# A fold of two weight matrices woven into attention: matmuls issued in pieces, sums moved out of PSUM later

## The chip, the cores and the metric

The kernel runs on one core of a Trainium2 chip. The core has five engines, each with its own in-order queue: TensorE (PE in the profile; PEld is its weight load), VectorE (DVE), ScalarE (ACT), GpSimd (POOL) and SyncE (SP), which issues the transfers here. TensorE writes its sums into PSUM, which ScalarE and VectorE read; all else is kept in SBUF. The metric is the device time of one execution in microseconds (us).

## The reference

The kernel computes three stages in a row on 2304 tokens of width 512.

```python
scores = scale * q @ k.T           # 4 batches x 8 heads, 576 tokens, head width 64, causal
a = softmax(scores)                # over the keys
local = a @ v
mem_out = (phi(q) @ M_prev) / (phi(q) . z_prev + 1e-6)
x = g * mem_out + (1 - g) * local  # g: one gate per head
x = ((x @ w1) * (x @ w2)) @ w3 @ w_out     # 512 -> 1024 -> 1024 -> 512
h = x @ w_in                               # 512 -> 2048
x = (h - tanh(h)) @ w_out2                 # 2048 -> 512
```

The weights w1, w2, w3, w_out, w_in and w_out2 arrive as 64-bit numbers.

## The kernel before

**Decoding.** A tile of weights is loaded as 64-bit words (`dec_load`) and turned into fp32 by `dec_ops`: one ScalarE pass (L74), four VectorE passes (L75, L77, L81, L84), and then a split into a high and a low part by two GpSimd passes (L96, L99). Products of fp32 accuracy are made of three matmuls: high by high, high by low, low by high. `Decoder` hands out such a tile in five pieces, one for each call of `step`, and issues the load of a later tile when one is done.

**The fold.** Since nothing stands between w3 and w_out, the kernel multiplies them first: `fold_work` makes WF = w3 @ w_out while attention runs. It decodes eight tiles of w_out (`o`) and 16 tiles of w3 (`zs`, eight for each half of the 1024 rows). For each of eight row blocks and each half, 12 matmuls of 512 columns add into one PSUM bank (`fo`). In the first half ScalarE copies the sum to SBUF (`part`, L291). In the second half VectorE adds that part (`s`, L294), ScalarE copies the rounded sum (`wf`, L296) and VectorE subtracts to get the low part (L297). The bank comes from the pool `psA`, whose two banks attention's outputs (`o`, in `av`) use too.

**Attention.** There are 80 units: 16 pairs of heads, five blocks of queries each. The outer loop (`for m in range(NU + 8)`) issues for each step, in the order of ORDER, the scores, exponentials and normalization of unit m (S, E, N), the transposes of unit m - 1 (T), some preparation of the next pair (L), the background work (G, three steps behind), and the outputs (A, two steps behind, after the second and the fifth unit of a pair).

**Background work.** `early()` is a generator that runs the fold, and then the first memory group (`mem_group(0)`) interleaved with the decoding of the first four tiles of w1 and w2: after each memory step come two decoder steps. G gives it a budget: BG = 2.13 in the first 40 steps and BG2 = 2.09 in the others are added to a counter, and each piece that is not a `yield 1` takes one from it. The fold yields 1 after each three matmuls, so these cost nothing and the 12 matmuls of a fold are issued within one step, with the sum's way out of PSUM right behind them. Eight pieces are issued before the first step.

The framework that the kernel is written in takes this order as a priority. It places each instruction on its engine's queue when a simulation of the timeline finds it ready, so pieces of the background can be issued a little ahead or behind; on the chip each engine then keeps to its queue's order.

**After attention.** The products with w1 and w2 (`ab`) and with WF (`x`) follow in six groups of 384 tokens, beside the other memory groups and the rest of the decoding, and then the third stage in the same groups.

Of the kernel before, what the change touches and what calls it, by code (L numbers as in the profile page):

```python
# [11 lines left out]
F32 = mybir.dt.float32  # L12
# [5 lines left out]
AF = mybir.ActivationFunctionType  # L18
ALU = mybir.AluOpType
# [13 lines left out]
def block_kernel(ctx, tc, qk, qt, vt, mp, zp_d, beta, w1, w2, w3t, wo, wi, wo2, ident_d, mask_d, out):  # L33
    nc = tc.nc
    PE, DV, AC, PO, SP = nc.tensor, nc.vector, nc.scalar, nc.gpsimd, nc.sync
# [3 lines left out]
    wfp = ctx.enter_context(tc.tile_pool(name="wfp", bufs=1))  # L39
# [15 lines left out]
    def wslot(pool, tag, dt=F32R):  # L55
        return pool.tile([128, 2, 512], dt, tag=tag, name=tag if dt == F32R else tag + "p")
# [110 lines left out]
    OP, FL = 5, "V"  # L167
    SN, XP, MR = 2, (), 0
    TH = (("V", 0), ("A", 0))
    PS = 1  # L170
    U1 = 2
    NE, EM, BG = 4, 1, 2.13
    BG2, MB = 2.09, 40
    MS, FS, FS5 = 4, 3, 12
    CPA = (0, 1, 3, 4)

# [57 lines left out]
    WF = {}  # L234
# [16 lines left out]

    def fold_item(f, half):
        def dst():
            t = wslot(ap1, "zs")
            fv[f, half] = t
            return t[:, 0], t[:, 1]

        r = slice(512 * half, 512 * half + 512)
        return w3t[r, f * 128:f * 128 + 128].rearrange("(k p) c -> p k c", p=128), dst

    def fold_work(psum):
        seq = [("o", j) for j in range(4)]
        for f in range(8):
            if f >= OP:
                seq += [("o", 4 + f - OP)] if 4 + f - OP < 8 else []
            seq.append((f, 0))
        seq += [("o", j) for j in range(12 - OP, 8)]
        for f in range(8):
            seq += [("x", i) for i, x in enumerate(XP) if x == f]
            seq.append((f, 1))  # L270
        make = {"o": fold_o_item, "x": lambda i: w_items[i]}
        dec = Decoder([make[k[0]](k[1]) if k[0] in make else fold_item(*k) for k in seq], DW, 3)
        part = {}
        for half in range(2):
            for f in range(8):
                while dec.done <= seq.index((f, half)) or half and dec.done <= seq.index(("o", 7)):
                    dec.step()
                    yield
                acc = psum()
                t = fv.pop((f, half))  # L280
                for j in range(4):
                    o = FO[4 * half + j]
                    c = slice(128 * j, 128 * j + 128)
                    mm(acc, t[:, 0, c], o[:, 0], j == 0, False)
                    mm(acc, t[:, 0, c], o[:, 1], False, False)
                    mm(acc, t[:, 1, c], o[:, 0], False, j == 3)
                    if j % FG == FG - 1:
                        yield 1
                if half == 0:
                    part[f] = wslot(wfp, f"wf{f}", F32)  # L290
                    AC.activation(out=part[f][:, 0], in_=acc, func=AF.Copy)  # L291
                else:
                    s = ap1.tile([128, 512], F32, tag=f"s{f % SN}", name="s")
                    DV.tensor_tensor(out=s, in0=acc, in1=part[f][:, 0], op=ALU.add)  # L294
                    WF[f] = wslot(wfp, f"wf{f}")
                    AC.activation(out=WF[f][:, 0], in_=s, func=AF.Copy)  # L296
                    (DV if FL == "V" else PO).tensor_tensor(out=WF[f][:, 1], in0=s, in1=WF[f][:, 0].bitcast(F32),  # L297
                                                            op=ALU.subtract)
                    yield 2

    if True:
        load_qk(0)
# [336 lines left out]
        def do(x, n):  # L639
            nonlocal pp  # L640
            if not 0 <= n < NU:
                return
            P, u = units[n]
            if x == "S":
                if u == 0 and P >= 2:
                    run(pp)
                for y in range(2):
                    scores(n, y)
                    rmax(n, y)
            elif x == "E":  # L650
                for y in range(2):
                    exps(n, y)
            elif x == "N":
                norm(n)
            elif x == "T":
                trans(n)
            elif x == "A" and u in (1, 4):
                av(P, u // 4)
                if u == 4 and P + 2 < 16:
                    load_v(P + 2)  # L660
            elif x == "L":
                if u == 0 and P >= 1:
                    run(pp)
                    pp = prep_qk(P + 1) if P + 1 < 16 else iter(())
                for _ in range(PS):
                    next(pp, None)
            elif x == "G":
                bgc[0] += BG if n < MB else BG2
                with ExitStack() as s:
                    for e, k in TH:  # L670
                        if n - k >= 0:
                            s.enter_context(tc.issue_after(mark[e][n - k]))
                    while bgc[0] >= 1:
                        if next(bg, None) != 1:
                            bgc[0] -= 1

        for m in range(NU + 8):
            for x in ORDER:
# [361 lines left out]
```

## Time and profile before

The median of three runs is 1062.15 us (1060.85 to 1065.14). The profiled execution took 1062.19 us; its span, from the first to the last instruction, is 1060.4 us, and the mean granted TensorE clock 0.975 of full speed.

| engine | busy us | share of the span | instructions |
|---|---|---|---|
| TensorE | 987.8 | 93% | 5512 |
| TensorE weight load | 860.3 | 81% | 5512 |
| VectorE | 821.7 | 77% | 1465 |
| ScalarE | 609.5 | 57% | 1413 |
| GpSimd | 442.4 | 42% | 446 |

Busy time is the union of an engine's instructions, averaged over stages with different limits. Matmuls overlap, so TensorE's busy time isn't its work at full speed. A wait is put down to the instruction that released it last.

### The profile page before, as it was taken

The numbers are of one execution on the slowest core, as the hardware profiler recorded it, in microseconds if no ns is written. First come the engines' busy times: TensorE is split into PE (matmuls) and PEld (weight loads), VectorE is DVE, ScalarE is ACT, GpSimd is POOL, SyncE is SP. The second block draws the span as 40 slices with busy tenths as digits, with TensorE's granted clock in tenths as the row PEclk, the third lists the DMA queues.
The fourth block names the chain that finished last, engine by engine and source line by source line (L and its number), as shares of the span: only waits on it lengthen the run. The fifth ranks groups of instructions, "written<-read, shape, count | busy, mean of one in ns | idle before, by whom it ended". The sixth has DMA issues, their size and how long they took to land.

```text
span 1060.4 us, 15816 instructions
## 1 busy us (share of the span) xinstructions
PE 987.8 (93%) x5512; PEld 860.3 (81%) x5512; DVE 821.7 (77%) x1465; ACT 609.5 (57%) x1413; POOL 442.4 (42%) x446
## 2 busy tenths in 40 slices
PE   5799898978899899999999997999999999999998
PEld 3476666655588789999999987789999999999996
DVE  7989998999879995467121498988778787787875
ACT  5577676666732432324121534777777776776764
POOL 5788777778646423100000584622222222222221
PEclk8699999998999899999999998999999999999999
DMA  9764675543324451125000022000000000000000
GB/s 246 182 174 123 173 196 136 135 126 95 94 73 152 137 177 50 41 88 160 1 1 1 20 74 86 1 1 30 1 1 30 1 31 1 1 31 1 31 1 30
DMA packets 44415, 77.73 MB, mean 73 GB/s; under 512 B 5168, under 2 KB 30000, under 8 KB 42416
## 3 DMA queue, kind: packets, MB, share of 16 engines
q1 hardware_dynamic: 44336, 76.73, 26.0%
q8 instruction: 43, 0.70, 0.3%
q14 instruction: 36, 0.29, 0.1%
HBM read 72.00 MB, written 4.72 MB: 72 GB/s over the span
## 4 chain that ended last, share of the span: by engine, by line
PE 66%; DVE 22%; POOL 6%; issue 4%; ACT 2%; DMA 1%; SPq 0%; DVEq 0%; POOLq 0%; ACTq 0%
PE o L143 20%; PE h L143 18%; PE ab L143 14%; PE x L143 7%; DVE T L81 3%; PE sc L143 2%; DVE T L75 2%; DVE T L84 2%; DVE st L394 2%; POOL p L427 2%; DVE qs L224 2%; PE t L459 1%; DVE T L77 1%; DVE ks L226 1%; PE fo L143 1%
## 5 line engine op out<-in xcount | busy, mean ns | idle before, releaser
L922 POOL TENSOR_TENSOR gl<-s,gh 128x384 fp32r<-128x384 f32 x96 | 102.0, 1062 | 286.0 <-ACT gh L916 267.7
L427 POOL TENSOR_SCALAR p<-p,st 128x128 f32<-128x128 f32 (+2 forms) x144 | 111.6, 787 | 52.2 <-DVE st L420 25.5
L143 PE MATMUL ab<-xh,wa 128*128 128x384 f32 x384 | 109.8, 343 | 5.0 <-DVE a L723 2.0
L143 PE MATMUL ab<-xh,wb 128*128 128x384 f32 x384 | 108.5, 340 | 2.8 <-POOL wb L96 2.0
L143 PE MATMUL x<-abh,wf 128*128 128x384 f32 x384 | 108.4, 343 | 1.6 <-ACT abh L726 1.6
L143 PE MATMUL sc<-ks,qs 128*128 128x256 f32 (+4 forms) x384 | 92.0, 358 | 18.2 <-DVE qs L224 9.5
L898 DVE SCALAR_TENSOR_TENSOR s<-s,u 128x384 f32<-128x384 f32 x96 | 82.2, 857 | 23.6 <-ACT s L888 22.8
L407 ACT ACTIVATE p<-sc,st 128x256 f32<-128x256 f32 (+4 forms) x160 | 82.6, 527 | 31.2 <-DVE st L394 13.3
L723 DVE TENSOR_TENSOR a<-ab,a 128x384 f32<-128x384 f32 x48 | 26.5, 553 | 86.2 <-PE ab L143 73.5
L894 ACT ACTIVATE u<-u,pc 128x384 f32<-128x384 f32 x96 | 59.3, 620 | 43.6 <-DVE s L898 43.5
L143 PEld LDWEIGHTS sc<-ks,qs 128*128 128x128 f32 x384 | 63.3, 205 | 25.5 <-ACT p L407 9.6
L74 ACT ACTIVATE T<-raw 128x512 f32<-128x512 f32 x72 | 48.8, 678 | 55.9 <-POOL wb L99 9.2
L143 PEld LDWEIGHTS ab<-xh,wa 128*128 128x128 f32 x384 | 70.5, 189 | 10.0 <-issue 3.3
L904 DVE TENSOR_TENSOR t<-h,t 128x384 f32<-128x384 f32 x96 | 53.1, 553 | 30.1 <-ACT t L887 29.7
L143 PEld LDWEIGHTS ab<-xh,wb 128*128 128x128 f32 x384 | 71.1, 190 | 4.5 <-POOL wb L96 2.7
L459 PE MATMUL t<-ident,p 128*128 128x128 f32 x320 | 54.6, 291 | 21.4 <-POOL p L427 8.2
L143 PEld LDWEIGHTS x<-abh,wf 128*128 128x128 f32 x384 | 71.3, 191 | 2.9 <-ACT abh L726 2.5
L903 DVE SCALAR_TENSOR_TENSOR s<-s,s 128x384 f32<-128x384 f32 x96 | 65.5, 682 | 7.9
L886 ACT ACTIVATE u<-h 128x384 f32<-128x384 f32 x96 | 46.8, 488 | 40.8 <-PE h L143 40.8
L143 PE MATMUL x<-abl,wf 128*128 128x384 f32 x192 | 65.6, 341 | 3.3 <-DVE abl L727 3.3
L143 PE MATMUL h<-xh,wf 128*128 128x384 f32 x240 | 67.5, 342 | 1.0 <-DVE s L905 1.0
L96 POOL TENSOR_SCALAR wb<-T 128x512 fp32r<-128x512 f32 x12 | 8.5, 709 | 142.4 <-PE ab L143 134.5
(205 smaller groups left out, 2865.0 us busy)
## 6 DMA issues: line engine op xcount, KB each, us to landing
r<-in_qk SPq DMA_DIRECT2D x30, 576.0 KB, 7.4
raw<-in_wo SPq DMA_DIRECT2D x24, 512.0 KB, 3.6
raw<-in_w3t SPq DMA_DIRECT2D x16, 512.0 KB, 4.9
raw<-in_w SPq DMA_DIRECT2D x16, 512.0 KB, 3.7
raw<-in_wi SPq DMA_DIRECT2D x16, 512.0 KB, 3.7
v<-in_vt SPq DMA_DIRECT2D x16, 320.0 KB, 6.0
mw<-in_qt SPq DMA_DIRECT2D x18, 256.0 KB, 3.0
out<-ob SPq DMA_DIRECT2D x18, 256.0 KB, 2.3
```

What stands on the lines that cost most here:

```text
L74: AC.activation(out=tf, in_=hw.bitcast(F32), func=AF.Abs)
L81: DV.scalar_tensor_tensor(out=l16, in0=lw, scalar=2.0 ** -29, in1=l16, op0=ALU.mult, op1=ALU.add)
L143: return PE.matmul(o, lhsT, rhs, start=start, stop=stop).ins
L407: mark["A"][n] = AC.activation(out=p_t[n][:, o:o + w], in_=sc_t.pop((n, x))[:, 0:w], func=AF.Exp, bias=st[:, b:b + 1], accum_out=st[:, 2 + ...
L427: (DV if NV[u] == "V" else PO).tensor_scalar(out=pr, in0=pr, scalar1=sc, scalar2=1.0, op0=ALU.mult, op1=ALU.mult)
L459: PE.transpose(t[:, m], p[:, K * h + 128 * kb:K * h + 128 * kb + 128], ident)
L886: AC.activation(out=u, in_=o, func=AF.Square)
L894: AC.activation(out=u, in_=u, func=AF.Relu, bias=pc[:, 2:3])
L898: DV.scalar_tensor_tensor(out=s1, in0=s1, scalar=k2[0], in1=u, op0=ALU.add, op1=ALU.mult)
L903: DV.scalar_tensor_tensor(out=s1, in0=s2, scalar=k2[1], in1=s1, op0=ALU.add, op1=ALU.mult)
L904: DV.tensor_tensor(out=t, in0=o, in1=t, op=ALU.subtract)
L922: PO.tensor_tensor(out=l, in0=s1, in1=h[:].bitcast(F32), op=ALU.subtract)
```

## The change

The fold's matmuls, still yielding 1 after each three, now take half a unit of the budget each, and one more piece follows the last of them. A sum is no longer taken out of PSUM right behind its matmuls: it is put on a list (`behind`), and `leave_step` issues one instruction of the oldest entry after each later decoder step: the copy of the first half is one such step, the add, the rounded copy and the subtract of the second half are three. When the decoding is over, the rest of the list is issued one piece at a time. The decoded w3 tile `zs` comes from a pool of two buffers (`ap2`) instead of one. Both budgets rise to 2.75. `mem_setup`, called at `yield 2`, now runs once, at the end of the fold.

```diff
--- before.py
+++ after.py
@@ -169,8 +169,8 @@
     TH = (("V", 0), ("A", 0))
     PS = 1
     U1 = 2
-    NE, EM, BG = 4, 1, 2.13
-    BG2, MB = 2.09, 40
+    NE, EM, BG = 4, 1, 2.75
+    BG2, MB = 2.75, 40
     MS, FS, FS5 = 4, 3, 12
     CPA = (0, 1, 3, 4)
 
@@ -251,7 +251,7 @@
 
     def fold_item(f, half):
         def dst():
-            t = wslot(ap1, "zs")
+            t = wslot(ap2, "zs")
             fv[f, half] = t
             return t[:, 0], t[:, 1]
 
@@ -271,10 +271,30 @@
         make = {"o": fold_o_item, "x": lambda i: w_items[i]}
         dec = Decoder([make[k[0]](k[1]) if k[0] in make else fold_item(*k) for k in seq], DW, 3)
         part = {}
+        behind = deque()
+
+        def leave(half, f, acc):
+            if half == 0:
+                part[f] = wslot(wfp, f"wf{f}", F32)
+                AC.activation(out=part[f][:, 0], in_=acc, func=AF.Copy)
+                return
+            s = ap1.tile([128, 512], F32, tag=f"s{f % SN}", name="s")
+            DV.tensor_tensor(out=s, in0=acc, in1=part[f][:, 0], op=ALU.add)
+            yield
+            WF[f] = wslot(wfp, f"wf{f}")
+            AC.activation(out=WF[f][:, 0], in_=s, func=AF.Copy)
+            yield
+            DV.tensor_tensor(out=WF[f][:, 1], in0=s, in1=WF[f][:, 0].bitcast(F32), op=ALU.subtract)
+
+        def leave_step():
+            if behind and next(behind[0], behind) is behind:
+                behind.popleft()
+
         for half in range(2):
             for f in range(8):
                 while dec.done <= seq.index((f, half)) or half and dec.done <= seq.index(("o", 7)):
                     dec.step()
+                    leave_step()
                     yield
                 acc = psum()
                 t = fv.pop((f, half))
@@ -286,17 +306,12 @@
                     mm(acc, t[:, 1, c], o[:, 0], False, j == 3)
                     if j % FG == FG - 1:
                         yield 1
-                if half == 0:
-                    part[f] = wslot(wfp, f"wf{f}", F32)
-                    AC.activation(out=part[f][:, 0], in_=acc, func=AF.Copy)
-                else:
-                    s = ap1.tile([128, 512], F32, tag=f"s{f % SN}", name="s")
-                    DV.tensor_tensor(out=s, in0=acc, in1=part[f][:, 0], op=ALU.add)
-                    WF[f] = wslot(wfp, f"wf{f}")
-                    AC.activation(out=WF[f][:, 0], in_=s, func=AF.Copy)
-                    (DV if FL == "V" else PO).tensor_tensor(out=WF[f][:, 1], in0=s, in1=WF[f][:, 0].bitcast(F32),
-                                                            op=ALU.subtract)
-                    yield 2
+                yield
+                behind.append(leave(half, f, acc))
+        while behind:
+            leave_step()
+            yield
+        yield 2
 
     if True:
         load_qk(0)
@@ -671,8 +686,7 @@
                         if n - k >= 0:
                             s.enter_context(tc.issue_after(mark[e][n - k]))
                     while bgc[0] >= 1:
-                        if next(bg, None) != 1:
-                            bgc[0] -= 1
+                        bgc[0] -= 0.5 if next(bg, None) == 1 else 1
 
         for m in range(NU + 8):
             for x in ORDER:
```

## Rows read from the trace of the kernel before

**Rows 1.** Busy time by stretch: PE, PEld, DVE, ACT, POOL, clock, DMA.

```profile
...
52.60:230.00 177.40, 158.23 (x1040) 117.31 (x1039) 166.70 (x343) 121.86 (x344) 139.82 (x154) 0.98 0.59 151
200.00:250.00 50.00, 40.29 (x259) 28.83 (x260) 49.72 (x94) 32.68 (x92) 38.55 (x39) 0.93 0.49 120
230.00:285.00 55.00, 45.98 (x321) 31.84 (x321) 52.43 (x124) 42.37 (x126) 41.13 (x51) 0.94 0.43 113
300.00:400.00 100.00, 91.53 (x510) 81.30 (x509) 90.08 (x161) 37.35 (x75) 46.03 (x38) 0.95 0.45 137
500.00:550.00 50.00, 50.00 (x288) 50.00 (x287) 10.74 (x20) 11.40 (x24) 0.00 (x0) 1.00 0.00 1
...
```

**Rows 2.** Waits of VectorE, 52.6 to 230 us: total us, times, longest.

```profile
...
DVE g L440 <- PE t L466: 3.0, 2, 1.8
DVE st L394 <- PE sc L143: 2.0, 2, 1.5
DVE ks L226 <- POOL ks L208: 1.8, 4, 1.2
...
DVE st L416 <- ACT p L407: 1.1, 2, 0.7
```

**Rows 3.** Groups of VectorE, 52.6 to 230 us: busy us, mean ns, idle before.

```profile
...
L84 DVE SCALAR_TENSOR_TENSOR T<-raw,T 128x512 uint32<-128x512 uint32 x21 | 17.9, 853 | 0.1
L81 DVE SCALAR_TENSOR_TENSOR T<-raw,T 128x512 uint16<-128x512 uint32 x21 | 16.9, 802 | 0.0
...
L75 DVE TENSOR_SCALAR T<-T 128x512 f32<-128x512 f32 x21 | 12.1, 574 | 1.5 <-ACT T L74 1.3
...
L77 DVE TENSOR_SCALAR T<-T 128x512 uint32<-128x512 uint32 x21 | 11.2, 531 | 0.1
...
L297 DVE TENSOR_TENSOR wf<-s,wf 128x512 fp32r<-128x512 f32 x7 | 5.4, 766 | 0.3
...
L294 DVE TENSOR_TENSOR s<-fo,wf1p 128x512 f32<-128x512 f32 x1 | 0.7, 673 | 0.0
...
```

**Rows 4.** Groups of TensorE, same stretch: the fold's matmuls and attention's outputs.

```profile
...
L143 PE MATMUL o<-g,v 128*64 128x320 f32 (+4 forms) x274 | 32.6, 368 | 1.0 <-DVE g L440 0.9 <-ACT g L438 0.2
...
L143 PE MATMUL fo<-z,zs 128*128 128x512 f32 x96 | 26.1, 414 | 1.1 <-POOL zs L99 0.6 <-POOL zs L96 0.4
...
L143 PE MATMUL fo<-wa,zs 128*128 128x512 f32 x48 | 16.0, 425 | 6.6 <-POOL zs L96 4.4 <-DVE mst L562 2.1
L143 PE MATMUL fo<-wb,zs 128*128 128x512 f32 x48 | 14.0, 400 | 0.0
...
```

**Rows 5.** Timeline, 160 to 170 us: start, us, engine, what, idle before.

```profile
...
160.16 2.48 POOL L427 TENSOR_SCALAR p<-p,st 128x256 f32<-128x256 f32 x4 [1.35 <-PE sc L143]
...
162.61 0.61 POOL L96 TENSOR_SCALAR zs<-T 128x512 fp32r<-128x512 f32 x1
...
163.28 0.82 PE L143 MATMUL fo<-wa,zs 128*128 128x512 f32 x2 [2.81 <-POOL zs L96]
...
164.99 0.69 DVE L440 COPY g<-t 128x512 f32<-128x512 f32 x1 [1.76 <-PE t L466]
...
```

**Rows 6.** Waits of ScalarE, 145 to 230 us.

```profile
...
ACT wf L296 <- DVE s L294: 10.8, 7, 2.4
...
```

**Rows 7.** Timeline of TensorE, 273 to 300 us.

```profile
...
274.38 2.16 PE L143 MATMUL o<-g,v 128*64 128x320 f32 x16
...
285.18 2.42 PE L143 MATMUL o<-g,v 128*64 128x320 f32 x20
...
291.90 0.44 PE L143 MATMUL ab<-xh,wa 128*128 128x384 f32 x1
...
```

**Rows 8.** Durations ns, min/median/max: the fold's subtract; GpSimd's second split pass.

```profile
...
L297 DVE TENSOR_TENSOR wf<-s,wf x8: 669/680/1100, 161.3 to 234.5; 128x512 fp32r<-128x512 f32 x8
...
L99 POOL TENSOR_TENSOR zs<-T,zs x16: 1267/1290/1648, 51.1 to 216.2; 128x512 fp32r<-128x512 f32 x16
...
```

**Rows 9.** DMA issues: count, KB each, us from issue to landing.

```profile
...
raw<-in_w3t SPq DMA_DIRECT2D x16, 512.0 KB, 4.9
...
```

## The prediction

> **What bounds the kernel now.** I read four views in this order. First the page's busy times, then busy time by stretch, because the page's average hides that the stages have different limits. From 500 us on TensorE is busy 50.00 of 50 us and VectorE only 10.74 [rows 1]: whatever happens earlier moves the end one for one, and nothing of the change lies in that part. The changed code (the fold and what is scheduled with it) runs from 52.6 to 230 us. There VectorE is busy 166.70 of 177.40 us, TensorE 158.23, ScalarE 121.86, GpSimd 139.82; from 230 to 285 us, where attention ends beside the first decoding of w1 and w2 and the first memory group, VectorE is busy 52.43 of 55.00 [rows 1]. So VectorE sets the pace until about 285 us, TensorE is close behind it, and the time there is VectorE's work plus VectorE's idle time: 10.7 us idle in the fold's stretch (177.40 - 166.70), 2.6 us after it. From 300 to 400 us TensorE is busy 91.53 and VectorE 90.08 of 100 us; that stage gets the same work either way.
>
> Second, the waits of VectorE in the fold's stretch. What a fold can cause is 3.0 us for copies `g` behind transposes and 2.0 us for row maxima `st` behind scores, 5.0 us together; the 1.8 us behind GpSimd's `ks` and 1.1 us behind an exponential have nothing of the fold in them [rows 2]. Third, the operations themselves: four VectorE passes for each decoded tile, and for the second half of the fold one add (0.7 us) and one subtract (0.766 us) [rows 3]; the fold's own matmuls, 26.1 + 16.0 + 14.0 = 56.1 us of TensorE, with idle time before them of 1.1 + 6.6 + 0 = 7.7 us, most of it ended by GpSimd's `zs` [rows 4]. Fourth, one such stall in order of time, to see whether it reaches VectorE: GpSimd normalizes from 160.16 us (2.48 us), so the split of `zs` starts only at 162.61, the fold's first two matmuls wait 2.81 us at the head of TensorE's queue, and the transposes queued behind them come late, so that VectorE's copy at 164.99 waits 1.76 us [rows 5]. That is the chain that the change can cut.
>
> **How often each thing is issued.** The background work gets a budget for each attention step (80 steps). Before: 2.13 units (2.09 later), five units a decoded tile, the fold's matmuls free. 24 tiles are 120 units, 8 are spent ahead, so the fold ends (112 - 40 x 2.13) / 2.09 = 12.8 steps after the first 40: about step 53 of the background, 56 in the outer count. Between the first fold (outer step 11) and the last (56) lie 45 steps, 177.4 / 45 = 3.94 us each. After: each fold costs 4 x 0.5 + 1 = 3 units more, 16 x 3 = 48, so (168 - 8) / 2.75 = 58.2 steps, outer step 61. The rest (18 rounds of one memory step and two decoder steps, 54 units, and three units for the last sum) takes 57 / 2.75 = 20.7 steps instead of 54 / 2.09 = 25.8, so both end at outer step 82. Walking the counters by hand, the last two matmul pieces of the first memory group are issued at steps 78 and 80 instead of 77 and 79. Nine of the 16 folds get their twelve matmuls split over two steps; seven are still issued within one step. In eleven folds the first matmuls are issued in the very step that splits their own `zs` (ten before).
>
> **What it costs, part by part.** No instruction is added or removed on any engine, so VectorE's 166.70 + 52.43 us of work stay; what can move is idle time.
>
> *Matmuls three at a time.* The 5.0 us above are the whole gain that the trace shows for this [rows 2]. Bounds: 0 (all stalls stay, since eleven folds still start in the step of their own `zs`) to 5.0. I take half, 2.5 us, as nine of 16 are split.
>
> *Sums that leave later.* ScalarE waits 10.8 us in seven places for the fold's add before its copy `wf` [rows 6]. After the change the copy is issued a unit after the add, and the subtract a unit after that, so this wait should go. It is worth little: ScalarE is busy 121.86 of 177.40 us, and the only wait of VectorE on ScalarE's exponentials is 1.1 us [rows 2]. Bounds: 1.1 us gained, 1.1 us lost (a sum that now sits between two decoder passes can delay them as well); I take 0. Behind the add in VectorE's queue stand decoder passes and attention's row maxima; it is issued a step after the matmuls that it waits for, so it should find them done. The bank of PSUM is held one or two steps longer, some 4 to 8 us. Two banks serve the fold and attention's outputs in turn; by the same walk every sum is out at least a step before its bank's next user, so I price this at 0: the other bank hides it.
>
> *Two buffers for `zs`.* No wait of GpSimd for a free `zs` shows: the split's idle time is put down to other things, and the folds wait for the data, not GpSimd for the buffer [rows 4, 5]. Gain 0; if the next split came while the matmuls still read, one buffer would cost GpSimd at most a fold's length, 56.1 / 16 = 3.5 us.
>
> *Rates.* The fold's stretch gets four more attention steps and less decoding in each, the stretch after it four fewer. If VectorE stays the bound this is neutral: without the decoder's 17.9 + 16.9 + 12.1 + 11.2 and the sums' 5.4 + 8 x 0.673 us [rows 3] its other work is (166.70 - 68.9) / 45 = 2.17 us a step, and what one stretch gains the other loses. The loads move with the decoder: the first of w1 is issued at outer step 62 instead of 56, and its ScalarE pass in the same step. A load of this kind takes 4.9 us to land [rows 9], more than a step, but the scheduler places the pass by readiness as it does before the change; I price it at 0, and at one load, 4.9 us, if ScalarE's queue stands still for it.
>
> *Hand-over.* The w1 and w2 matmuls start at 291.90 us, behind the last of the first memory group; the attention outputs of the last two pairs before it, at 274.38 and 285.18, are five steps apart, so a step is 10.8 / 5 = 2.2 us there [rows 7]. Issued one step later, the first group costs 0 (TensorE has attention's tail to do) to 2.2 us. I take 1.0.
>
> Sum: -2.5 + 0 + 0 + 0 + 1.0 = -1.5 us. The profiled execution took 1062.19 us for a span of 1060.4 us, within 0.1 us of the median of the runs, 1062.15. So 1062.2 - 1.5 = 1060.7 us. Bounds of this case: -5.0 - 1.1 = -6.1 and +1.1 + 2.2 = +3.3, so 1056 to 1065.5 us.
>
> **Rivals.**
> *All the idle time goes.* From 200 to 250 us VectorE is busy 49.72 of 50.00 us [rows 1], so the engine can run almost without gaps. If smoother TensorE queues give that over the fold's stretch, idle falls from 10.7 to 177.4 x 0.28 / 50 = 1.0 us: -9.7, with the hand-over +1.0: -8.7, 1053.5 us. For it: TensorE is busy 89% of this stretch, so a lump of 12 matmuls is hard to catch up. Against it: half of VectorE's waits come from elsewhere.
>
> *Steps don't get shorter (slower).* If a step's 3.94 us is set by the chain from scores to outputs rather than by VectorE's work, taking decoding out of it doesn't shorten it. Then four more steps cost 4 x 3.94 = 15.8 us before the fold ends, and the stretch after it, with VectorE at 95%, wins back only 4 x 2.17 = 8.7: +7.1 us, 1069.3 us. It decides when VectorE's busy share in the fold's stretch falls below some 90%. Against it: 94% now.
>
> *VectorE and GpSimd stretch each other.* The subtract takes 669 ns at least and 1100 at most, and GpSimd's longest pass beside it 1290 ns in the middle [rows 8]. A subtract set apart from its sum may land beside GpSimd's passes each time: 8 x 0.43 = 3.4 us at most, 1064.1 with the sum above. The Trainium skill ("SBUF — State Buffer", who interferes with whom) makes the shared port pair an exclusive lock: a VectorE instruction with two SBUF inputs waits for the whole GpSimd instruction. By that each of the eight could lose 1.29 us, 10.3 in all, 1071; the stretched 1100 ns agree with the lock but show a third of its price.
>
> *A held bank stops TensorE.* If VectorE or ScalarE run a unit late with the sums, attention's next output stands at the head of TensorE's queue until the bank is free. A unit is 3.94 / 2.75 = 1.4 us; for each of 16 sums that is 22.9 us, 1083.6 with the sum above. Against it: before, the 274 output matmuls waited 1.0 us in all, and for their own `g`, not for a bank [rows 4], and the count leaves a step of room. The Trainium skill ("PSUM — Partial Sum Buffer", summary of rules for kernel authors) speaks for it: it says to evacuate promptly, PSUM being tight. No row of before shows a late sum that could confirm it.
>
> *It does not do what it says.* Seven folds keep their lump and eleven their own `zs`; were the scheduler to put the rest back together too, nothing changes: 1062.2 us.
>
> **How the numbers follow.** Forecast 0.47, all idle time 0.30, steps not shorter 0.11, stretching 0.05, held bank 0.04, nothing 0.03. A difference under 0.5%, 5.3 us, is about what a measurement of this kernel can tell from none, so faster is below 1056.8 and slower above 1067.5. Faster: 0.28 of the second case and 0.04 of the forecast, 0.32. Slower: 0.10 of the third, 0.01 of the fourth and the held bank's 0.04, 0.15. Same: 0.53. The range reaches to 1051 and 1069.
>
> **What would show it.** Right: the fold's idle time on TensorE below 7.7 us, ScalarE's 10.8 us wait for the add gone, VectorE's waits behind transposes and scores down to some 2.5 us, the w1 and w2 matmuls starting at 289 to 292 us. Wrong: VectorE's busy share of the fold's stretch well under 94% (steps not shorter), outputs of attention waiting for a fold's bank, or decoder passes and subtracts longer than in rows 3 and 8.

## The result, and the profile after

The changed kernel takes 1073.89 us (median; 1072.17 to 1074.73) against 1062.05 us for the kernel before in the same comparison. The ratio is 1.0096, 95% interval [1.0074, 1.0118]. It is slower by about 1%, above the range of the prediction. The profiled execution took 1074.59 us for a span of 1072.8 us, 12.4 us more than the span before.

First: where along the span is it lost? Cut both traces at the last row maximum of attention (VectorE's last `st<-sc`) and at the first product with w1 (`ab`). Busy time by stretch, kernel before, then kernel after (PE, PEld, DVE, ACT, POOL, then granted clock, DMA share, GB/s):

```profile
0.00:283.22 283.22, 234.95 (x1500) 170.18 (x1501) 260.82 (x539) 191.51 (x541) 215.50 (x247) 0.94 0.61 156
283.22:291.90 8.68, 8.21 (x61) 4.46 (x60) 5.43 (x14) 6.46 (x19) 3.64 (x5) 1.00 0.11 30
...
52.60:250.00 197.40, 173.48 (x1134) 127.62 (x1133) 186.54 (x381) 135.81 (x385) 154.64 (x169) 0.97 0.59 151
```

```profile
0.00:290.33 290.33, 240.69 (x1503) 173.24 (x1503) 260.92 (x538) 190.85 (x540) 205.42 (x247) 0.92 0.60 152
290.33:304.00 13.67, 11.72 (x70) 6.13 (x69) 6.11 (x16) 7.29 (x20) 4.09 (x5) 0.88 0.05 20
...
52.60:250.00 197.40, 175.46 (x1140) 128.19 (x1138) 179.28 (x377) 134.84 (x384) 140.64 (x166) 0.96 0.58 148
```

The third column of numbers is the one to read. Up to the last row maximum VectorE works 260.82 us before and 260.92 us after: the same. But that point comes at 290.33 instead of 283.22 us, 7.1 us later, so all of it is idle time of VectorE (22.4 us before, 29.4 after). From there to `ab` it takes 13.67 instead of 8.68 us, another 5.0. The remaining part is 768.8 us (1072.8 - 304.0) against 768.5 (1060.4 - 291.9). So the whole loss, 12.1 us, lies before `ab`: 7.1 in attention, 5.0 in the hand-over. From 52.6 to 250 us VectorE's busy share falls from 94.5% (186.54 / 197.40) to 90.8%; over the prediction's stretch, 52.6 to 230 us, from 94.0 to 89.9% (159.47 / 177.40). From 52.6 to 250 us both kernels begin 88 row maxima, but the kernel after begins 83 decoder passes instead of 90: the time that the decoder left free did not bring attention forward.

Second: what does VectorE wait for now? Its waits of the kernel after from 52.6 to 230 us, which answer to [rows 2] (total us, times, longest):

```profile
DVE ks L226 <- POOL ks L208: 5.8, 4, 2.4
DVE st L409 <- PE sc L143: 5.7, 5, 3.2
DVE st L431 <- ACT p L422: 3.1, 3, 1.9
DVE g L455 <- PE t L474: 0.5, 2, 0.3
```

The fold's matmuls in the kernel after, 50 to 238 us, answering to [rows 4], busy us, mean ns and idle time before them:

```profile
L143 PE MATMUL fo<-z,zs 128*128 128x512 f32 x96 | 27.3, 426 | 0.0
L143 PE MATMUL fo<-wa,zs 128*128 128x512 f32 x48 | 14.8, 413 | 0.0
L143 PE MATMUL fo<-wb,zs 128*128 128x512 f32 x48 | 14.0, 396 | 0.0
```

The chain that the prediction wanted cut is cut: the fold waits 0.0 us on TensorE instead of 7.7, and VectorE's copies `g` wait 0.5 us instead of 3.0. But the waits for scores, for GpSimd's `ks` and for the exponentials rose from 4.9 to 14.6 us together. The largest rise, 4.0 us, is that behind `ks`, which GpSimd makes and no fold does.

Third: one such place in order of time. VectorE of the kernel after; L75, L77, L81 and L84 are the decoder's passes:

```profile
95.75 0.78 DVE L81 SCALAR_TENSOR_TENSOR T<-raw,T 128x512 uint16<-128x512 uint32 x1
...
97.43 0.67 DVE L84 SCALAR_TENSOR_TENSOR T<-raw,T 128x512 uint32<-128x512 uint32 x1
98.03 0.14 DVE L435 RECIPROCAL st<-st 128x2 f32<-128x2 f32 x1
99.28 0.49 DVE L409 TENSOR_REDUCE st<-sc 128x1 f32<-128x320 f32 x1 [1.11 <-PE sc L143]
100.60 0.42 DVE L409 TENSOR_REDUCE st<-sc 128x1 f32<-128x256 f32 x1 [0.83 <-PE sc L143]
...
105.77 0.40 DVE L75 TENSOR_SCALAR T<-T 128x512 f32<-128x512 f32 x1
...
119.12 1.58 DVE L409 TENSOR_REDUCE st<-sc 128x1 f32<-128x512 f32 x3 [3.19 <-PE sc L143]
```

TensorE of the kernel after at the same times:

```profile
95.54 3.05 PE L143 MATMUL fo<-z,zs 128*128 128x512 f32 x12
98.43 1.23 PE L143 MATMUL sc<-ks,qs 128*128 128x320 f32 x8
...
114.59 2.38 PE L143 MATMUL fo<-z,zs 128*128 128x512 f32 x9
...
117.17 0.94 PE L143 MATMUL fo<-z,zs 128*128 128x512 f32 x3
...
118.53 0.48 PE L143 MATMUL sc<-ks,qs 128*128 128x512 f32 x1
```

The fold occupies TensorE for 3 us, the scores queue behind it, and the row maxima come late. VectorE's last decoder pass ends at 98.1 us, the next begins at 105.77. The same place in the kernel before, VectorE and then TensorE:

```profile
97.82 0.95 DVE L84 SCALAR_TENSOR_TENSOR T<-raw,T 128x512 uint32<-128x512 uint32 x1
98.69 0.81 DVE L394 TENSOR_REDUCE st<-sc 128x1 f32<-128x320 f32 x2
...
106.05 0.83 DVE L75 TENSOR_SCALAR T<-T 128x512 f32<-128x512 f32 x1
```

```profile
93.02 2.61 PE L143 MATMUL fo<-z,zs 128*128 128x512 f32 x10 [0.64 <-POOL zs L99]
...
95.82 1.30 PE L143 MATMUL sc<-ks,qs 128*128 128x320 f32 x8
```

There too a fold stands in front of the scores, and there too no decoder pass follows for 7.3 us. But there the scores are done before the decoder passes are, and the stretch holds 0.35 us of idle time instead of 2.06. From 40 to 245 us both kernels have eight stretches of over 5 us between two decoder passes, 66.6 us in all before and 66.8 after; the idle time in them is 6.4 and 12.8 us. So the time without a decoder pass did not grow; what VectorE has to wait for within it did. Note the 12 matmuls in one block at 95.54: the four pieces of a fold can still stand in a row on TensorE.

### The profile page after: what moved, and what is told of

Its sections match the earlier page's. It is cut to its first block, busy times and chain, and to the rows that moved or that the text cites. A ratio compares the mean times of both kernels' runs of the same rounds, so it can differ in the third digit from the quotient of the medians.

```text
span 1072.8 us, 15840 instructions
## 1 busy us (share of the span) xinstructions
PE 995.8 (93%) x5512; PEld 865.8 (81%) x5512; DVE 822.2 (77%) x1465; ACT 609.0 (57%) x1413; POOL 430.9 (40%) x446
## 4 chain that ended last, share of the span: by engine, by line
PE 67%; DVE 19%; DMA 4%; issue 3%; POOL 3%; ACT 2%; SPq 0%; DVEq 0%; POOLq 0%; ACTq 0%
PE o L143 21%; PE h L143 18%; PE ab L143 14%; PE x L143 7%; DVE T L81 3%; PE sc L143 3%; DVE qs L224 2%; DMA mw<-in_qt 2%; DVE T L84 2%; PE fo L143 2%; DVE T L75 2%; PE t L474 2%; DMA r<-in_qk 1%; DVE T L77 1%; DVE st L409 1%
## 5 line engine op out<-in xcount | busy, mean ns | idle before, releaser
L442 POOL TENSOR_SCALAR p<-p,st 128x128 f32<-128x128 f32 (+2 forms) x144 | 101.9, 720 | 54.4 <-DVE st L435 28.8
```

Source lines behind the costliest of these rows:

```text
L442: (DV if NV[u] == "V" else PO).tensor_scalar(out=pr, in0=pr, scalar1=sc, scalar2=1.0, op0=ALU.mult, op1=ALU.mult)
```

## The experiments

Theories, as the expectations call them. **Theory 1**: while a fold's pieces take budget, no decoder pass reaches VectorE, and it idles behind TensorE. **Theory 2**: the sums that leave late cost (a held bank, a late weight). **Theory 3**: the hand-over's 5 us are a loss of their own, since the first memory group comes late. **Theory 4**: the order that the scheduler finds for a given pace decides.

Every kernel was timed in five rounds beside the kernel before. The last three columns are worked out from each profiled execution as above: VectorE's idle time up to the last row maximum, when that comes, and when the first `ab` starts, in us. A profiled execution can differ from its kernel's median: those of e5, e7, e10 and e18 took 2.2 to 4.0 us more, those of e1 and e4 1.8 and 2.0 us less.

| kernel | median us | ratio, 95% interval | idle | last row max | `ab` |
|---|---|---|---|---|---|
| before (first comparison) | 1062.05 | | 22.4 | 283.2 | 291.9 |
| after (first comparison) | 1073.89 | 1.0096 [1.0074, 1.0118] | 29.4 | 290.3 | 304.0 |
| e1_free | 1066.98 | 1.0039 [1.0025, 1.0054] | 21.6 | 284.7 | 293.5 |
| e2_now | 1071.68 | 1.0088 [1.0067, 1.0109] | 30.4 | 290.7 | 300.8 |
| e3_buf | 1060.88 | 0.9979 [0.9969, 0.9989] | 19.9 | 283.3 | 292.0 |
| e4_beside | 1069.47 | 1.0063 [1.0043, 1.0084] | 21.5 | 285.8 | 294.6 |
| e5_mem | 1072.42 | 1.0095 [1.0073, 1.0117] | 29.8 | 289.7 | 299.4 |
| e6_price1 | 1072.09 | 1.0094 [1.0081, 1.0107] | 23.2 | 284.5 | 299.9 |
| e7_pace | 1070.25 | 1.0068 [1.0053, 1.0083] | 29.8 | 290.8 | 298.5 |
| e8_beside_now | 1063.65 | 1.0009 [1.0000, 1.0017] | 20.2 | 283.8 | 292.5 |
| e9_after_slow | 1070.51 | 1.0089 [1.0070, 1.0109] | 24.3 | 288.5 | 300.9 |
| e10_after_fast | 1071.37 | 1.0098 [1.0082, 1.0114] | 27.3 | 291.2 | 304.7 |
| e11_before_slow | 1064.22 | 1.0024 [1.0014, 1.0034] | 25.2 | 284.6 | 293.3 |
| e12_before_fast | 1069.74 | 1.0073 [1.0061, 1.0085] | 24.5 | 288.8 | 296.6 |
| e13_beside_late | 1066.41 | 1.0036 [1.0023, 1.0048] | 20.0 | 284.9 | 295.3 |
| e14_late | 1066.24 | 1.0036 [1.0024, 1.0048] | 20.8 | 285.2 | 295.4 |
| e15_priced_once | 1065.81 | 1.0031 [1.0019, 1.0043] | 21.6 | 285.5 | 294.7 |
| e16_one_buf | 1070.45 | 1.0075 [1.0058, 1.0092] | 26.2 | 289.0 | 301.1 |
| e17_late_short | 1060.44 | 0.9986 [0.9976, 0.9995] | 18.6 | 281.9 | 290.7 |
| e18_after_short | 1071.98 | 1.0099 [1.0083, 1.0115] | 28.6 | 291.2 | 301.2 |

### Undoing the change part by part

**e1_free**: the changed kernel, the fold's matmuls free again.

```diff
-    NE, EM, BG = 4, 1, 2.75
-    BG2, MB = 2.75, 40
+    NE, EM, BG = 4, 1, 2.13
+    BG2, MB = 2.2, 40
...
-                yield
                 behind.append(leave(half, f, acc))
...
-                        bgc[0] -= 0.5 if next(bg, None) == 1 else 1
+                        if next(bg, None) != 1:
+                            bgc[0] -= 1
```

> The changed kernel with the price of the matmuls undone: pieces of three are free again and no piece follows them, so the twelve matmuls of a fold are issued in one step; sums still leave one to three pieces later, zs keeps two buffers. Budgets 2.13 and 2.2, so that the fold and the first memory group end where they did before. Theory 1 (while a fold's pieces take budget, no decoder pass reaches VectorE, and it idles behind TensorE): back to before, 1059 to 1065 us, VectorE's idle time from 0 us to the last score near 22 us instead of 29. Theory 2 (the late sums or the bank that they hold cause the loss): stays at 1071 to 1076 us.

The idle time falls to 21.6 us, below that of the kernel before, and more than half of the loss is gone; the time lies between the ranges of the two theories. What stays, +0.39%, was not explained by this run (see e14 and e17).

**e2_now**: the changed kernel, every sum leaving at once.

```diff
-                behind.append(leave(half, f, acc))
+                run(leave(half, f, acc))
```

> The changed kernel with its sums taken out at once, as before the change; the price of the matmuls, the budgets of 2.75 and two buffers for zs stay. Theory 1: 1068 to 1075 us, the idle time of VectorE between 63 and 140 us stays 8 us or more above that of before. Theory 2: back to 1060 to 1066 us.

Still +0.88% and 30.4 us idle: the late sums are not the main cause.

**e3_buf**: the kernel before with two buffers for `zs`.

```diff
-            t = wslot(ap1, "zs")
+            t = wslot(ap2, "zs")
```

> The kernel before with two buffers for zs, nothing else. It tells apart the 4 us that stayed when the matmuls were free again: if the late sums cost them, 1060 to 1064 us here; if the second buffer does (by another order that the scheduler finds), 1065 to 1068 us.

A little faster than the kernel before, with an interval below 1. The fold's matmuls of e3, 48 to 240 us, stop waiting with this edit alone:

```profile
L143 PE MATMUL fo<-z,zs 128*128 128x512 f32 x96 | 26.3, 417 | 0.0
L143 PE MATMUL fo<-wa,zs 128*128 128x512 f32 x48 | 14.6, 409 | 0.0
L143 PE MATMUL fo<-wb,zs 128*128 128x512 f32 x48 | 13.6, 392 | 0.0
```

**e4_beside** and **e5_mem**: the changed kernel with a decoder pass issued beside each three matmuls; and with a faster background from step 58 on, so that the first memory group is not late.

```diff
 e4: BG = 2.25, BG2 = 2.25
-                    if j % FG == FG - 1:
-                        yield 1
-                yield
+                    dec.step()
+                    leave_step()
+                    yield
 e5:
-    BG2, MB = 2.75, 40
+    BG2, MB = 3.2, 58
```

> The changed kernel with one decoder pass issued beside each three matmuls, so that a piece has work for both engines; each piece costs one unit, none follows the matmuls; budgets 2.25. Sums still leave late, two buffers for zs. Theory 1: VectorE no longer runs dry in the fold: 1055 to 1063 us. Theory 2: 1070 us or more.

> The changed kernel with a budget of 3.2 instead of 2.75 from step 58 on, so that the first memory group is issued some two steps earlier. Theory 3 (of the 12 us, 5 are lost after the last score, because the first memory group is late and the w1 and w2 matmuls wait for it): 1067 to 1071 us, and the w1 and w2 matmuls start 9 us after the last row maximum as before, not 14. If only the fold's stretch matters: 1072 to 1076 us.

e4 brings the idle time to 21.5 us with the matmuls still in pieces, as Theory 1 has it, but keeps +0.63%, a time between the two ranges. e5 does shorten the hand-over (299.4 - 289.7 = 9.7 us instead of 13.7) and wins nothing. Waits of VectorE in e5, 285 to 330 us:

```profile
DVE a L737 <- ACT a L736: 8.5, 1, 8.5
```

In the kernel after, the wait for the first product in that stretch is 3.6 us. The work that came earlier waits for the same TensorE queue a little later. Theory 3 as a lever falls: in the priced kernel the hand-over is not a loss that can be taken back by itself.

### Is it the missing decoder pass?

**e8_beside_now**: as e4, with the sums at once and a pace of 2.13 and 2.2. **e6_price1**: the changed kernel with a whole unit for each three matmuls, pace 3.15. **e7_pace**: the kernel before at a pace of 2.2.

```diff
 e8: BG = 2.13, BG2 = 2.2
-                    if j % FG == FG - 1:
-                        yield 1
-                yield
-                behind.append(leave(half, f, acc))
+                    dec.step()
+                    yield
+                run(leave(half, f, acc))
 e6: BG = BG2 = 3.15
-                        bgc[0] -= 0.5 if next(bg, None) == 1 else 1
+                        next(bg, None)
+                        bgc[0] -= 1
 e7: BG = BG2 = 2.2
```

> One decoder pass beside each three matmuls, sums taken out at once, two buffers for zs, budgets 2.13 and 2.2. Theory 1: VectorE's idle time up to the last row maximum at most 22 us, 1058 to 1065 us. If a matmul lump cut in pieces is worth nothing or the second pass costs: 1066 to 1070 us, as the version with late sums.

> The changed kernel with a whole unit for each three matmuls instead of half a unit, budgets 3.15, so that the work still ends at step 82: decoder passes stand still for five units of ten instead of three of eight. Theory 1 (VectorE runs dry while the fold's pieces are taken): a larger dose, VectorE idle 32 us or more up to the last row maximum, 1076 to 1082 us. If the price only shifts the order by chance: 1068 to 1075 us.

> The kernel before with both budgets at 2.2 (2.13 and 2.09), nothing else: how much another pace of the same background moves the time by itself. Theory 1 and all rivals: 1059 to 1065 us. Beyond that the differences of 4 us among the runs would be the scheduler's chance.

e8 and e2 both issue the matmuls in pieces and the sums at once. In e8 each piece brings a decoder pass, in e2 it brings none. Busy time of e2, then of e8, up to the last row maximum and from there to `ab`:

```profile
0.00:290.70 290.70, 240.10 (x1497) 172.32 (x1498) 260.33 (x538) 189.77 (x538) 204.20 (x245) 0.92 0.60 152
290.70:300.80 10.10, 8.76 (x61) 4.54 (x59) 5.76 (x16) 7.59 (x20) 4.52 (x6) 1.00 0.10 26
```

```profile
0.00:283.80 283.80, 236.69 (x1500) 170.83 (x1501) 263.57 (x539) 191.83 (x541) 218.51 (x247) 0.93 0.60 156
283.80:292.50 8.70, 8.22 (x61) 4.47 (x60) 5.45 (x15) 6.43 (x19) 3.66 (x5) 1.00 0.11 30
```

VectorE idles 30.4 us in one and 20.2 in the other, though up to that point the same instructions take it 3.2 us longer in e8. So matmuls in pieces do no harm here if each brings a decoder pass. (The two also differ in pace.) The larger dose of e6 was a miss for Theory 1: the time does not grow with it, and lies in the range given for a price that only shifts the order by chance. Its idle time before the last row maximum is even 23.2 us, and its loss sits in the hand-over (15.4 us from the last row maximum to `ab`). e7 was the surprise: the kernel before, with nothing changed but a pace 3 to 5% faster, loses 0.68%, outside the range given to Theory 1 and all rivals, and idles 29.8 us as the changed kernel does, with no matmul priced.

### How much is the pace?

Two paces each for the kernel after (e9, e10) and the kernel before (e11, e12):

```diff
 e9:  BG = 2.65, BG2 = 2.9
 e10: BG = 2.85, BG2 = 2.7
 e11: BG = 2.08, BG2 = 2.17
 e12: BG = 2.18, BG2 = 2.06
```

> The changed kernel with budgets 2.65 and 2.9 instead of 2.75 twice: the same end at step 82, a slower start. Theory 1 (the price of the matmul pieces empties VectorE at any pace): 1069 to 1076 us. Theory 4 (the order that the scheduler finds for a pace decides, and 2.75 was an unlucky one): the four paces of this call spread over 1060 to 1072 us for both kernels alike.

> The changed kernel with budgets 2.85 and 2.7: the same end, a faster start. Theory 1: 1069 to 1076 us. Theory 4: anywhere from 1060 to 1072 us.

> The kernel before with budgets 2.08 and 2.17 instead of 2.13 and 2.09: the same end, a slower start. Theory 1: 1060 to 1066 us, under every changed kernel. Theory 4: anywhere from 1060 to 1072 us, as 2.2 twice took 1070.

> The kernel before with budgets 2.18 and 2.06: the same end, a faster start. Theory 1: 1060 to 1066 us. Theory 4: anywhere from 1060 to 1072 us.

The changed kernel stays between +0.89 and +0.98% at three paces. The kernel before is at its best at its own pace and loses 0.24 to 0.73% with a tenth of a unit more or less; e12, like e7, lies outside the range of Theory 1. So part of any difference here is the placement that a pace happens to give (Theory 4), and only kernels of one pace can be compared closely. Nor is the loss always idle time: e9 idles only 1.9 us more than the kernel before up to the last row maximum, and waits 0.4 us for scores from 52.6 to 230 us, but its VectorE work takes 264.2 us instead of 260.8 for the same instructions. Theory 1's "behind TensorE" does not hold there.

### Late sums, dose, buffer

**e13_beside_late** is e8 with the late sums added. **e14_late** is the kernel before, at its own pace, with two buffers and the late sums. **e15_priced_once** charges half a unit for each piece but has no piece behind the last, with the sums at once and a pace of 2.53. **e16_one_buf** is the changed kernel with one buffer.

```diff
 e13, against e8:
                     dec.step()
+                    leave_step()
                     yield
-                run(leave(half, f, acc))
+                behind.append(leave(half, f, acc))
 e14, against the kernel after: BG = 2.13, BG2 = 2.09
-                yield
                 behind.append(leave(half, f, acc))
...
-                        bgc[0] -= 0.5 if next(bg, None) == 1 else 1
+                        if next(bg, None) != 1:
+                            bgc[0] -= 1
 e15, against the kernel after: BG = BG2 = 2.53
-                yield
-                behind.append(leave(half, f, acc))
+                run(leave(half, f, acc))
 e16, against the kernel after:
-            t = wslot(ap2, "zs")
+            t = wslot(ap1, "zs")
```

> e8_beside_now (decoder pass beside each three matmuls, two buffers, pace 2.13 and 2.2: 1063.65 us, +0.7 against the kernel before) with the late sums of the change added. Theory 1 (the decoder standing still during the pieces is the loss): 1061 to 1066 us, VectorE idle before the last row maximum about 20 us. Theory 2 (late sums cost): 1067 to 1070, as e4_beside (1069.5), with idle before the last row maximum over 24 us or the w1 and w2 matmuls starting 3 us or more later than in e8.

> The kernel before with the late sums and two buffers, matmuls free, at its own pace 2.13 and 2.09. Theory 1 and 4 (e1_free's +4.8 us came from its later pace of 2.2): 1060 to 1064 us. Theory 2 (late sums cost by themselves): 1065 to 1068, idle of VectorE before the last row maximum over 24 us.

> The changed kernel with 0.5 unit for each three matmuls, no piece of its own after them, the sums at once, pace 2.53: two units without a decoder pass per fold instead of three. Theory 1: between the free kernels and the changed one, 1066 to 1071 us, VectorE idle before the last row maximum 25 to 29 us, about two thirds of the idle time in stretches without a decoder pass. Theory 2 and 4: 1061 to 1065, since the sums leave at once.

> The changed kernel with one buffer for decoded w3. All theories so far: 1072 to 1076 us, since the buffers have no part in the loss; if the second buffer lets GpSimd's splits run ahead at a bad moment in company of the price, under 1070.

e13 landed between what the two theories gave and e14 in the range of Theory 2: the late sums cost 0.27% beside e8 and 0.57% beside e3. But VectorE's idle time before the last row maximum, which Theory 2 wanted over 24 us, is what it was (20.0 against 20.2, 20.8 against 19.9 us). What moved is the end: `ab` starts 2.8 us later than in e8, and 3.3 later than in e3 (1.1 and 1.9 us of it lie before the last row maximum). e15 came out between the ranges, at 1065.81 us, with 21.6 us idle instead of the 25 to 29 of Theory 1: against e2, a third off the dose, at another pace, took away two thirds of the loss. e16 came out at 1070.45 us, between its two ranges; its interval overlaps that of the changed kernel, so no part of the second buffer in the loss is shown.

### The last sum's three steps

When the decoding is over, the last sum's three steps stand as units of their own ahead of the memory group. **e17_late_short** takes these out of e14, **e18_after_short** out of the changed kernel; all other sums leave as late.

```diff
         while behind:
             leave_step()
-            yield
         yield 2
```

> e14_late (the kernel before with late sums and two buffers, 1066.24 us, +3.6) with the last sum leaving in one go, so that no units stand between it and the first memory group; all other sums leave as late as in e14. Hand-over theory: the third transposes of the memory group back from 289.6 to 284 to 286 us, the w1 and w2 matmuls at 291 to 293 us, 1060 to 1063 us. If late sums cost by themselves (a held bank, a later weight): 1065 to 1067 as e14.

> The changed kernel with the last sum leaving in one go. Hand-over theory: the w1 and w2 matmuls from 304.0 to 299 to 302 us, 1069 to 1072 us: the part of the loss before the last row maximum (7 us) stays. If the hand-over is set by attention's last pieces and not by the units: 1073 to 1075.

TensorE of e14 and of e17 from the memory group's third transposes (`mt`) to `ab`:

```profile
289.63 0.60 PE L584 MATMUL mt<-ident,mw 128*128 128x128 f32 x4
...
295.37 0.42 PE L143 MATMUL ab<-xh,wa 128*128 128x384 f32 x1
```

```profile
283.37 0.66 PE L583 MATMUL mt<-ident,mw 128*128 128x128 f32 x4
...
290.68 0.44 PE L143 MATMUL ab<-xh,wa 128*128 128x384 f32 x1
```

Three units of 2.09 per step, 1.4 steps, were the whole cost of the late sums: without them `ab` starts 4.7 us earlier and the time falls by 5.8 us, to a little less than the kernel before. (3.3 of the 4.7 us lie before the last row maximum.) The sums themselves may be late for nothing. In the changed kernel the same edit starts `ab` 2.8 us earlier (301.2 instead of 304.0), but from there to the end it takes 772.2 us instead of 768.8 in the profiled execution, which was 3.2 us above e18's median. The median, 1071.98 us, is in the hand-over theory's range, but the ratio stays (1.0099 against 1.0096): no gain is shown, as in e5.

e17 and e18 ran side by side and differ only in what a matmul piece costs (nothing, or half a unit and one more per fold) and in the pace that makes up for it. Busy time of e17, then of e18:

```profile
0.00:281.90 281.90, 238.63 (x1500) 173.40 (x1501) 263.30 (x538) 192.25 (x540) 213.34 (x247) 0.92 0.61 157
```

```profile
0.00:291.20 291.20, 243.67 (x1498) 173.04 (x1499) 262.65 (x539) 190.15 (x538) 203.55 (x245) 0.91 0.58 152
```

Equal work (263.30 and 262.65 us), 18.6 against 28.6 us idle, 11.5 us of time. Taking all stretches over 5 us between two decoder passes on VectorE from 40 to 245 us, the idle time inside them is 2.8 us in e17 and 12.1 in e18 (6.4 before, 12.8 after); outside them it is 6.0 us in both. So the whole difference of that stretch lies where no decoder pass is at hand. These stretches make 49 us in all in e17 and 71 us in e18; with all over 2 us taken, 99 and 100 us. The same place on VectorE, the row maxima of one pair's last unit, first in e17, then in e18:

```profile
95.44 0.58 DVE L75 TENSOR_SCALAR T<-T 128x512 f32<-128x512 f32 x1
96.06 0.69 DVE L77 TENSOR_SCALAR T<-T 128x512 uint32<-128x512 uint32 x1
96.79 1.00 DVE L81 SCALAR_TENSOR_TENSOR T<-raw,T 128x512 uint16<-128x512 uint32 x1
97.83 0.69 DVE L84 SCALAR_TENSOR_TENSOR T<-raw,T 128x512 uint32<-128x512 uint32 x1
98.44 0.81 DVE L407 TENSOR_REDUCE st<-sc 128x1 f32<-128x320 f32 x2
```

```profile
97.08 0.69 DVE L84 SCALAR_TENSOR_TENSOR T<-raw,T 128x512 uint32<-128x512 uint32 x1
97.68 0.17 DVE L434 RECIPROCAL st<-st 128x2 f32<-128x2 f32 x1
99.51 0.49 DVE L408 TENSOR_REDUCE st<-sc 128x1 f32<-128x320 f32 x1 [1.67 <-PE sc L143]
100.83 0.42 DVE L408 TENSOR_REDUCE st<-sc 128x1 f32<-128x256 f32 x1 [0.82 <-PE sc L143]
```

In e17 a whole tile's passes fill the time until the scores are there, and the row maxima follow without a gap. In e18 the passes are used up and VectorE waits 2.5 us in two places.

## Why the prediction was wrong, by its own steps

**Rates: the step that failed.** It said that taking decoding out of the fold's stretch is neutral "if VectorE stays the bound", and took that as given from a busy share of 94% [rows 1]. Measured, VectorE's work stayed equal and 7.1 us of idle time came in. The count was close: going by the row maxima, 52.5 steps begin between the first and the last of the fold's matmuls instead of 47.5 (five more; the prediction's own 56 and 61 are five apart as well, but it reckoned with four). But these steps take 3.54 us (185.9 / 52.5) instead of 3.58 (170.1 / 47.5; the prediction had 3.94), hardly shorter, though each has less decoding in it. Neutral would have been 5 x 2.17 = 10.9 us more for this stretch; it took 15.8 more. VectorE was busy because the decoder filled the time in which attention's chain through TensorE, GpSimd and ScalarE was not ready; without the filler, what shows is that chain. The Trainium skill ("Perfetto Trace Analysis", Identifying the Most-Contended Engine) ranks engines by occupancy, and VectorE is that engine in this stretch, before and after; its occupancy did not tell whether its work can be moved for nothing, which was the question here.

**The rival "steps don't get shorter"** had the mechanism. That its size, +7.1 us, is also the measured one is in part luck: it reckoned with four more steps of 3.94 us, where the trace has five of 3.54. It had a chance of 0.11 and a point of decision "some 90%"; over the prediction's stretch the share measured is 89.9%, so this sign only just shows. With the hand-over's 5.0 us measured, its 1062.2 + 7.1 becomes 1074.3 us; the profiled execution took 1074.59.

**Hand-over: mis-sized.** Predicted +1.0 (0 to 2.2) with `ab` at 289 to 292 us; measured +5.0, with `ab` at 304.0. The three units of the last sum are in the prediction's count, as a step of 2.2 us; e14 and e17 price them at 5.8 us of time where nothing else is changed. In the changed kernel no worth of theirs is shown (e18). And 1.5 of the 5.0 us are attention's last 20 outputs, which took 3.90 us instead of 2.42 at a lower granted clock (last section); the prediction has no such term.

**Matmuls three at a time: right sign, wrong edit.** The idle time before the fold's matmuls went from 7.7 to 0.0 us and the wait for transposes from 3.0 to 0.5 [rows 2, 4]. But e3 shows the first with the second buffer alone, and cutting the matmuls in pieces adds no gain to that (e8 1.0009, at a slightly faster pace, and e3 0.9979).

**Two buffers: priced 0, worth -2.1 us** (e3, 0.21%). The prediction looked for a wait of GpSimd for a free buffer and found none; the buffer's gain showed as the fold's wait for GpSimd's `zs` in [rows 4], put down there to late data. In the changed kernel the second buffer shows no such gain (e16 with one buffer 1.0075, the changed kernel 1.0096).

**Late sums: 0, right** (e17 beside e3: 0.9986 and 0.9979). That holds for the sums themselves; the last one's three units belong to the hand-over. The reason given was partly wrong: ScalarE's wait for the add is not gone. Waits of ScalarE in the kernel after, 50 to 238 us, answering to [rows 6]:

```profile
ACT wf L285 <- DVE s L282: 8.9, 5, 4.4
```

The Trainium skill ("PSUM — Partial Sum Buffer", summary of rules for kernel authors) asks to evacuate promptly; in e17, with two banks in turn and a sum up to three pieces late, no cost shows. In the kernel after, none of the waits of TensorE from 50 to 238 us that the trace lists is one of attention's outputs. The rival of the held bank falls with it.

**VectorE and GpSimd stretching each other** shows no loss in the sum: VectorE's work up to the last row maximum is the same before and after. In its parts it moved: the passes for `qs`, which read two tiles in SBUF as the subtract does, took 35.4 us there instead of 31.3, those for `st` 109.0 instead of 117.0. In e17, the fastest, `qs` took 33.8, so most of that rise does not go with the time. The eight subtracts last 854 ns in the mean after and 952 in e17, the faster of the two, against 755 before. But a single one can be stretched as that rival has it. The longest subtract of e17, and GpSimd's pass at that time:

```profile
209.23 1.92 DVE L287 TENSOR_TENSOR wf<-s,wf 128x512 fp32r<-128x512 f32 x1
...
208.98 1.61 POOL L226 TENSOR_TENSOR ks<-r,ks 128x576 fp32r<-128x576 f32 x1
```

It begins 0.25 us after GpSimd's pass and ends some 0.55 us after that pass has ended; e17's shortest subtract takes 0.67 us in all. (A subtract of 1.30 us in the kernel after ends 0.55 us after such a pass too.) By the Trainium skill's lock ("SBUF — State Buffer", who interferes with whom) a subtract can have to wait out a whole GpSimd pass, and this row agrees. It is one of eight, so the means rose by only 0.1 to 0.2 us.

**Loads: 0, as far as the trace shows.** VectorE's passes L75 wait 0.2 us for ScalarE's first pass, 1.3 before [rows 3].

**What stays open.** The loss of the priced kernels is not proportional to the dose: +0.31% for two units a fold (e15), +0.75 to +0.99% for three (after, e2, e5, e9, e10, e16, e18), +0.94% for five (e6, there in the hand-over). Why the kernel before loses 0.68 to 0.73% at a slightly faster pace was not run down; e7 has 11.0 us of idle time in stretches without a decoder pass, e12 only 6.8. So the share of the pace in the loss is open too. That the price costs is shown: of all kernels here those with three or more priced units a fold are the slowest, at five different paces (though e16, the least of them, is not told apart from e7 and e12). How much of the 0.96% it makes is not: by e17 and e18, whose paces differ, all of it; by an estimate from the table, the mean of the seven kernels with three units (+0.91%) less that of the kernel before at its three other paces (+0.55%), some 0.4%, the rest being the good placement that the kernel before had at its own pace.

## What to carry to other kernels

An engine that is 94% busy may owe that to filler: before moving background work between stretches, ask what the engine does in the time that the filler covers now, and price the chain that would then be seen. When background work is cut into pieces, let each piece carry work for the busiest engine (e8), and don't charge a budget for pieces that bring it none (e17 against e18: 1.1%, with a change of pace in it). Three units queued ahead of the last stage's first piece cost 5.8 us (e14 against e17), more than any other part of the change did by itself at that pace, so count what stands between the last background item and the hand-over.

## What the runs showed beside this

The mean granted TensorE clock does not go with the time here. Up to the last row maximum it is 0.94 before, 0.92 after and 0.92 in e17, the fastest of these. In the hand-over of the kernel after it does cost: from 292.6 to 295.9 us the granted clock is 0.50, the lower level of 1.2 GHz, after TensorE had been busy 1.4 of 3.4 us (288.5 to 291.9), and the same 20 outputs take 3.90 us instead of 2.42 [rows 7], in this row of TensorE:

```profile
291.87 3.90 PE L143 MATMUL o<-g,v 128*64 128x320 f32 x20 [0.44 <-ACT g L453]
```

And an order made by a list scheduler is sensitive: 2.18 and 2.06 units per step instead of 2.13 and 2.09, with the same instructions, moved the kernel before by 0.73%. e3 and e17 are faster than the kernel before, by 0.21 and 0.14%.
